# Modulation rows of the first layer norm in three blocks instead of four, with the last key group accumulating in the bank that holds their products

## Chip, cores, metric

One core of one Trainium2 chip runs the whole kernel. The metric is device time in microseconds (us), the median of a kernel's executions. The 27 executions of the kernel before that were run beside the experiments lie within 0.25% (838.13 to 840.25 us). "Span" is the time from the first to the last instruction in the profile of one execution; it is about 2 us shorter than the measured time (on average 1.80 us for the kernel before, 2.01 for the changed one).

## The reference, cut to what matters

```python
# x: 2048 x 1024 bf16; c: 1 x 1024; w_mod: 1024 x 6144; wqkv: 1024 x 3072
mod = (silu(c) @ w_mod).reshape(1, 6, 1, 1024)
sa, ca, ga, sb, cb, gb = (mod[:, i] for i in range(6))
h = layernorm(x) * (1 + ca) + sa          # needs two sixths of w_mod
q, k, v = split(h @ wqkv)                  # 32 heads of 32
x = x + ga * (linear_attention(phi(q), phi(k), v) @ wo)
h = layernorm(x) * (1 + cb) + sb
x = x + gb * ((silu(h @ w_gate) * (h @ w_up)) @ w_down)
```

The change concerns the first 31 us alone: from the first loads to the end of the K products of the first 512 rows of x.

## The kernel before

In this stretch one queue of loads brings, in this order, four tiles of x, the columns of `w_mod` for scale (`ca`) and shift (`sa`), and the K half of `wqkv`: 7 MiB. `w_mod` comes in four blocks ("phases") of 2, 3, 2 and 1 columns of 128. Each phase ends with a "row step", which turns its products into scale and shift, and with a scaling of the transposed x. Only then can the K products of these columns run. There are eight K groups (4 row tiles by 2 halves), each of which adds up 8 columns in a PSUM bank of its own.

```python
    PH = [(0, 2), (2, 5), (5, 7), (7, 8)]
    ...
    load_wme(0, 0, DC); load_wk(0, 2)
    load_wme(1, 0, 4); load_wme(1, 4, 8); load_wk(2, 3); load_wk(3, 5)
    load_wme(2, 0, 4); load_wme(2, 4, 8); load_wk(5, 6); load_wk(6, 7)
    load_wme(3, 0, DC); load_wk(7, 8)
    ...
    # 128x1 products into bank 7, column 2*cc + kind
    nc.tensor.matmul(bank[7][:, o:o + 1], lhsT=wme[:, j, col:col + P], rhs=scT[:, j:j + 1], ...)

    def mod_rows(c0, c1):
        nc.vector.tensor_copy(out=m1[:, 1, c0:c1], in_=bank[7][:, 2 * c0:2 * c1:2])
        nc.vector.tensor_copy(out=saT[:, c0:c1], in_=bank[7][:, 2 * c0 + 1:2 * c1 + 1:2])
        nc.vector.tensor_scalar_add(out=ca1T[:, c0:c1], in0=m1[:, 1, c0:c1], scalar1=1.0)
    ...
    kblk(range(7), 2)                     # groups 0-6, column 2
    kblk(range(7), 3)
    mod_mm(2, 0, 0, 4); mod_mm(2, 1, 0, 4)
    kblk(range(4), 4)
    mod_mm(2, 0, 4, 8); mod_mm(2, 1, 4, 8)
    mod_finish(2); modulate_phase(2)
    kblk(range(4, 7), 4); kblk(range(7), 5); kblk(range(4), 6)
    mod_mm(3, 0, 0, DC); mod_mm(3, 1, 0, DC)
    mod_finish(3); modulate_phase(3)
    spread(nc.vector, scT[:])
    kblk(range(4, 7), 6)
    for cc in range(7):                   # group 7 waits for bank 7 to be free of rows
        kblk((7,), cc)
    for g in range(8):
        kblk((g,), 7)
        k_evac(bank[g], *G[g])
    # then the V groups: banks 0, 1, 2, 3, 4, 0, ...
```

## Time and profile before

| | |
|---|---|
| time, median of 3 | 838.41 us (838.36 to 838.48) |
| span of the profiled execution | 837.0 us |
| first V product | 31.44 us |
| last phase-2 piece of w_mod landed | 22.93 us |
| last wk piece landed | 26.67 us |

Landings are read from the semaphore updates in the trace. First two lines of the page: the span, and the busy time, share and number of instructions of each engine.

```profile
span 837.0 us, 10504 instructions
...
PE 825.1 (99%) x4127; PEld 388.4 (46%) x4207; DVE 351.5 (42%) x660; ACT 150.9 (18%) x288; POOL 80.1 (10%) x147
```

TensorE (PE) is 99% busy, so all there is to win are the few microseconds in which it waits, and the waits that its trace names all come before the first V product's start at 31.44 us. The timeline of TensorE shows them (start, duration, line, shapes, count; in brackets the idle time before and what ended it). L271 is a K product, L367 a modulation product, L286 the first V product.

```profile
17.59 1.69 PE L271 MATMUL bank<-M,M 128*128 128x512 bf16 x7 [0.46 <-DVE M L253]
19.75 1.67 PE L271 MATMUL bank<-M,M 128*128 128x512 bf16 x7 [0.48 <-DMA M<-in_A_wqkv_dram]
...
22.52 0.81 PE L367 MATMUL bank<-scT,M 128*128 128x1 bf16 x16
...
24.24 2.55 PE L271 MATMUL bank<-M,M 128*128 128x512 bf16 x11 [0.24 <-DVE M L253]
26.63 0.54 PE L367 MATMUL bank<-scT,M 128*128 128x1 bf16 x16
27.03 4.04 PE L271 MATMUL bank<-M,M 128*128 128x512 bf16 x18
31.44 2.75 PE L286 MATMUL bank<-M,M 128*128 128x512 bf16 x11 [0.36 <-DVE M L268]
```

One matmul takes 0.38 us in the trace, but the next starts after 0.216 us, so the idle time in brackets is smaller than the time in which nothing was started.

The chain of waits (start, duration, what) is followed back from the end of the kernel:

```profile
14.85 8.09 DMA M<-in_w_mod_dram
...
22.98 0.37 PE bank L367 x8
...
23.37 0.16 DVE m L373
...
23.77 0.42 DVE M L253
...
24.24 2.55 PE bank L271 x11
26.79 0.38 PE bank L367 x16
27.17 2.41 PE bank L271 x11
...
30.69 0.70 DVE M L268
...
31.44 0.59 PE bank L286 x2
```

The chain runs through the landing of the last phase-2 piece of `w_mod` at 22.93 us, the row step (L373 to L375: 0.40 us from its start to the scaling, L253), the rest of the products, and the evacuation of bank 0, for which the first V product waits.

### The profile page before, as it was taken

What the parts mean: (1) busy time and instruction counts of PE and PEld (TensorE: products, weight loads), DVE (VectorE), ACT (ScalarE), POOL (GpSimd) and SP (SyncE); (2) the same over time, 40 slices, a digit from 0 to 9 for tenths busy, and PEclk for the clock granted to TensorE, in tenths of its full rate; (3) what the DMA queues carried; (4) which work ended last, traced back from release to release, by engine and by line L of the source; (5) the groups of instructions that cost most, each with busy time, mean ns of one, the idle gap of its engine ahead of it and who ended that gap; (6) DMA issues with size and microseconds to landing.
All of it is one profiled execution on the core that took longest, in us unless ns stands there. A gap on an engine that the chain in (4) does not pass through costs nothing.

```text
span 837.0 us, 10504 instructions
## 1 busy us (share of the span) xinstructions
PE 825.1 (99%) x4127; PEld 388.4 (46%) x4207; DVE 351.5 (42%) x660; ACT 150.9 (18%) x288; POOL 80.1 (10%) x147
## 2 busy tenths in 40 slices
PE   8999999999999999999999999999999999999998
PEld 4454544544444444444444444444444444444445
DVE  5678889788656655344552012222101111111011
ACT  4335533323211111111110001111000111100000
POOL 2034310032222223100000000000000000000000
PEclk9999999999999999999999999999999999999999
DMA  9987888155588987998884225555313555211220
GB/s 290 314 169 137 137 177 213 41 136 126 145 216 220 214 238 200 244 284 239 251 260 124 76 72 153 156 154 153 102 66 94 152 153 152 73 38 45 76 70 26
DMA packets 232625, 129.41 MB, mean 155 GB/s; under 512 B 89728, under 2 KB 218752, under 8 KB 232576
## 3 DMA queue, kind: packets, MB, share of 16 engines
q1 hardware_dynamic: 182224, 97.01, 42.7%
q10 hardware_dynamic: 48048, 23.34, 12.9%
q0 software_dynamic: 2304, 8.39, 2.6%
q8 instruction: 33, 0.54, 0.3%
q14 instruction: 16, 0.13, 0.1%
HBM read 95.42 MB, written 12.58 MB: 129 GB/s over the span
## 4 chain that ended last, share of the span: by engine, by line
PE 96%; SPq 2%; DMA 1%; issue 1%; DVE 0%; ACT 0%
PE bank L555 23%; PE bank L574 23%; PE bank L549 23%; PE bank L286 7%; PE bank L506 7%; PE bank L294 7%; PE bank L271 6%; DMA M<-in_w_mod_dram 1%; PE bank L479 1%; PE bank L303 1%; SPq L144 1%; SPq L147 1%; SPq L137 0%; PE bank L367 0%; DVE M L268 0%
## 5 line engine op out<-in xcount | busy, mean ns | idle before, releaser
L555 PE MATMUL bank<-M,M 128*128 128x512 bf16 x881 | 210.4, 379 | 0.8
L549 PE MATMUL bank<-M,M 128*128 128x512 bf16 x875 | 209.9, 379 | 1.1
L557 DVE TENSOR_TENSOR M<-bank,e 128x512 bf16<-128x512 f32 x112 | 77.5, 692 | 249.0 <-PE bank L555 237.5
L574 PE MATMUL bank<-M,M 128*128 128x512 bf16 (+2 forms) x715 | 146.9, 362 | 0.6
L552 ACT ACTIVATE e<-bank 128x512 f32<-128x512 f32 x112 | 66.8, 597 | 439.6 <-PE bank L549 404.5
L574 PEld LDWEIGHTS <-M 128*128 128x128 bf16 x952 | 90.9, 98 | 103.0
L555 PEld LDWEIGHTS <-M 128*128 128x128 bf16 x896 | 87.7, 98 | 105.7
L549 PEld LDWEIGHTS <-M 128*128 128x128 bf16 x896 | 87.3, 98 | 103.8
L577 DVE TENSOR_TENSOR M<-bank,M 128x512 bf16<-128x512 f32 (+2 forms) x34 | 22.5, 661 | 169.9 <-PE bank L574 153.8
L271 PE MATMUL bank<-M,M 128*128 128x512 bf16 x248 | 56.8, 379 | 2.6 <-DVE M L253 1.6
L506 PE MATMUL bank<-M,M 128*128 128x512 bf16 x251 | 57.6, 379 | 0.3
L294 PE MATMUL bank<-M,M 128*128 128x512 bf16 x248 | 56.6, 379 | 0.4
L286 PE MATMUL bank<-M,M 128*128 128x512 bf16 x251 | 55.6, 379 | 0.6 <-DVE M L268 0.4
L266 ACT ACTIVATE e<-bank 128x512 f32<-128x512 f32 x64 | 37.3, 596 | 91.7 <-PE bank L294 52.8
L574 PE MATMUL bank<-M 128*128 128x512 bf16 x219 | 50.7, 379 | 0.3
L268 DVE SCALAR_TENSOR_TENSOR M<-bank,e 128x512 bf16<-128x512 f32 x64 | 44.3, 692 | 3.9
L326 DVE CUSTOM_DVE_ANT_0 M<-M,sc_bc 128x1024 f32<-128x1024 bf16 x32 | 40.1, 1252 | 0.4
L286 PEld LDWEIGHTS <-M 128*128 128x128 bf16 x256 | 25.0, 98 | 30.8 <-issue 0.6
L506 PEld LDWEIGHTS <-M 128*128 128x128 bf16 x256 | 25.0, 98 | 29.8
L271 PEld LDWEIGHTS <-M 128*128 128x128 bf16 x256 | 24.1, 98 | 30.8 <-DVE M L253 3.3
L267 DVE TENSOR_SCALAR e<-e 128x512 f32<-128x512 f32 x64 | 29.0, 453 | 21.2 <-ACT e L266 21.2
L294 PEld LDWEIGHTS <-M 128*128 128x128 bf16 x256 | 24.6, 98 | 27.9
(71 smaller groups left out, 339.9 us busy)
## 6 DMA issues: line engine op xcount, KB each, us to landing
M<-in_B_w_gate_dram SPq DMA_DIRECT2D x56, 512.0 KB, 3.9
M<-in_B_w_up_dram SPq DMA_DIRECT2D x56, 512.0 KB, 4.9
x_scratch<-M POOLq DMA_DIRECT2D x16, 512.0 KB, 5.5
M<-x_scratch ACTq DMA_DIRECT2D x16, 512.0 KB, 3.5
M<-in_B_w_down_dram SPq DMA_DIRECT2D x6, 1024.0 KB, 8.3
M<-in_A_x_dram SPq DMA_DIRECT2D x16, 256.0 KB, 4.1
M<-in_A_wqkv_dram SPq DMA_DIRECT2D x4, 1024.0 KB, 11.1
M<-in_A_x_dram ACTq DMA_DIRECT2D x16, 256.0 KB, 4.0
```

Source lines behind the costliest of these rows:

```text
L266: nc.scalar.activation(out=e[:], in_=acc, func=ACT.Exp)
L268: nc.vector.scalar_tensor_tensor(out=dst, in0=acc, scalar=0.0, in1=e[:], op0=ALU.max, op1=ALU.add)
L271: nc.tensor.matmul(acc[:], lhsT=M4[:, sc_, cc, t * P:(t + 1) * P], rhs=wk[:, cc, h * NB:(h + 1) * NB], start=(cc == 0), stop=(cc == DC - 1))
L286: nc.tensor.matmul(acc[:], lhsT=M4[:, sc_, cc, t * P:(t + 1) * P], rhs=wv[:, cc, h * NB:(h + 1) * NB], start=(cc == 0), stop=(cc == DC - 1))
L294: nc.tensor.matmul(acc[:], lhsT=wq[:, cc, qc * P:(qc + 1) * P], rhs=M4[:, sc_, cc, :], start=(cc == 0), stop=(cc == DC - 1))
L326: nc.vector.tensor_tensor_reduce(out=prod.rearrange("p (j k) -> p j k", j=DC), in0=rowT[i][:, :, b, :], in1=sc_bc[:].rearrange("p (j k) -> ...
L506: nc.tensor.matmul(acc[:], lhsT=oTs[st % 3][:, cc, :], rhs=wo[:, cc, hs], start=(cc == 0), stop=(cc == DC - 1))
L549: nc.tensor.matmul(g_ps[:], lhsT=wg_blk[:, cc, fs], rhs=M4[:, sc_, cc, :], start=(cc == 0), stop=(cc == DC - 1))
L552: nc.scalar.activation(out=sg[:], in_=g_ps[:], func=ACT.Silu)
L555: nc.tensor.matmul(u_ps[:], lhsT=wu_blk[:, cc, fs], rhs=M4[:, sc_, cc, :], start=(cc == 0), stop=(cc == DC - 1))
L557: nc.vector.tensor_tensor(out=gus[sc_][:, f, :], in0=u_ps[:], in1=sg[:], op=ALU.mult)
L574: nc.tensor.matmul(y_ps[:, 0:w], lhsT=gus[sc_][:, f, t * P:(t + 1) * P], rhs=wd(f)[:, c0:c1], start=(f == 0), stop=(f == FC - 1))
```

## The change

Its intent: one row step less, no small last block, a shorter row step (one add in float32), K group 7 no longer left to the end but kept in step by sharing bank 7 with the modulation products, the last columns group by group so that evacuation starts early, and some products of zeros ("fill", "warm") in places where TensorE waits. The diff, cut to its core:

```diff
-    PH = [(0, 2), (2, 5), (5, 7), (7, 8)]
+    PH = [(0, 2), (2, 5), (5, 8)]
     ...
-    load_wk(3, 5)
+    load_wk(3, 4)
+    load_wk(4, 5)
     load_wme(2, 0, 4)
     load_wme(2, 4, 8)
     load_wk(5, 6)
-    load_wk(6, 7)
-    load_wme(3, 0, DC)
-    load_wk(7, 8)
+    load_wk(6, 8)
     ...                                   # one_zero: float32, 1 0 1 0 ...
+        nc.vector.tensor_tensor(out=modT[:, o0:o1], in0=bank[7][:, N7 + o0:N7 + o1], in1=one_zero[:, o0:o1], op=ALU.add)
     ...
+    def fill(n):                          # N7 = 384; zeros onto unused columns of bank 7
+        for _ in range(n):
+            nc.tensor.matmul(bank[7][:, N7 + 2 * DC:NB], lhsT=zt[:, 0:P], rhs=zt[:, N7 + 2 * DC:NB], ...)
+    def kmm7(cc, part):                   # group 7: 384 columns at once, the last 128 at the end
+        c0, c1 = (N7, NB) if part else (0, N7)
+        nc.tensor.matmul(bank[7][:, c0:c1], lhsT=M4[:, 0, cc, 3 * P:4 * P], rhs=wk[:, cc, NB + c0:NB + c1], ...)
     ...
+    kblk(range(8), 2)
+    kblk(range(8), 3)
+    kblk(range(3), 4)
     mod_mm(2, 0, 0, 4)
     mod_mm(2, 1, 0, 4)
-    kblk(range(4), 4)
+    kblk(range(3, 6), 4)
     mod_mm(2, 0, 4, 8)
+    fill(6)
     mod_mm(2, 1, 4, 8)
     mod_finish(2)
     modulate_phase(2)
     ...                                   # phase 3 and the late group 7 removed
+    kblk(range(6, 8), 4)
     for g in range(8):
-        kblk((g,), 7)
+        for cc in range(5, 8):
+            kblk((g,), cc)
+        if g == 7:
+            for cc in range(DC):
+                kmm7(cc, 1)
         k_evac(bank[g], *G[g])
```

Left out: the same treatment of phases 0 and 1, five added warm-up products, and the first normalization moved ahead of half of another tile's statistics.

More of the change, by code (lines that the diff above doesn't have):

```diff
@@ L176 @@
     nc.gpsimd.memset(den_eps_t[:], DEN_EPS)
-    saT = const.tile([P, DC], BF16, name="saT")
-    ca1T = const.tile([P, DC], BF16, name="ca1T")
+    modT = const.tile([P, 2 * DC], F32, name="modT")
+    ca1T, saT = modT[:, 0::2], modT[:, 1::2]
+    one_zero = const.tile([P, 2 * DC], F32, name="one_zero")
+    nc.gpsimd.memset(one_zero[:], 0.0)
+    nc.gpsimd.memset(one_zero[:, 0::2], 1.0)
     sbT = const.tile([P, DC], BF16, name="sbT")
@@ L359, in tr0_evac @@
             nc.vector.tensor_copy(out=dst, in_=tp)
+    N7 = 384
     def mod_mm(p, kind, j0, j1):
@@ L364, in mod_mm @@
             for cc in range(c0, c1):
-                o = (2 * cc) + kind
+                o = N7 + 2 * cc + kind
                 col = (0 if kind else D) + cc * P
                 nc.tensor.matmul(bank[7][:, o:o + 1], lhsT=wme[:, j, col:col + P], rhs=scT[:, j:j + 1],
-                                 start=(not kind and j == 0 and cc == c0),
-                                 stop=(kind == 1 and j == DC - 1 and cc == c1 - 1),
-                                 skip_group_check=True)
-    def mod_rows(c0, c1):
-        nc.vector.tensor_copy(out=m1[:, 1, c0:c1], in_=bank[7][:, 2 * c0:2 * c1:2])
-        nc.vector.tensor_copy(out=saT[:, c0:c1], in_=bank[7][:, 2 * c0 + 1:2 * c1 + 1:2])
-        nc.vector.tensor_scalar_add(out=ca1T[:, c0:c1], in0=m1[:, 1, c0:c1], scalar1=1.0)
-    def mod_finish(p):
-        mod_rows(*PH[p])
+                                 start=(p == 0 and kind == 0 and j == 0 and cc == c0),
+                                 stop=(kind == 1 and j == DC - 1 and cc == c1 - 1), skip_group_check=True)
+    def mod_finish(p):
+        o0, o1 = 2 * PH[p][0], 2 * PH[p][1]
+        nc.vector.tensor_tensor(out=modT[:, o0:o1], in0=bank[7][:, N7 + o0:N7 + o1], in1=one_zero[:, o0:o1], op=ALU.add)
+    def fill(n):
+        for _ in range(n):
+            nc.tensor.matmul(bank[7][:, N7 + 2 * DC:NB], lhsT=zt[:, 0:P], rhs=zt[:, N7 + 2 * DC:NB],
+                             start=False, stop=True, skip_group_check=True)
+    def kmm7(cc, part):
+        c0, c1 = (N7, NB) if part else (0, N7)
+        nc.tensor.matmul(bank[7][:, c0:c1], lhsT=M4[:, 0, cc, 3 * P:4 * P], rhs=wk[:, cc, NB + c0:NB + c1],
+                         start=(part == 1 and cc == 0), stop=(cc == DC - 1), skip_group_check=True)
     def modulate_phase(p, c0=0, c1=SCW):
@@ L393 @@
     ln_stats_act(1)
-    ln_stats(2)
-    ln_xn(0, nc.vector)
+    ln_stats(2, lambda: ln_xn(0, nc.vector))
     tr0(0)
     tr0_evac(0)
-    warm(2)
+    warm(4)
     ln_stats(3, lambda: ln_xn(1, nc.vector))
@@ L402 @@
     ln_xn(2, nc.vector)
+    warm(2)
     mod_mm(0, 0, 0, DC)
@@ L407 @@
     tr0_evac(2)
+    warm(1)
     modulate_phase(0, 0, 2 * P)
@@ L419, in kblk @@
         for g in gs:
-            kmm(bank[g], 0, G[g][0], G[g][1], cc)
+            if g < 7:
+                kmm(bank[g], 0, G[g][0], G[g][1], cc)
+            else:
+                kmm7(cc, 0)
     kblk(range(4), 0)
-    kblk(range(1), 1)
     tr0(3)
+    modulate_phase(0, 2 * P, 3 * P)
     tr0_evac(3)
-    kblk(range(1, 4), 1)
-    modulate_phase(0, 2 * P, 4 * P)
+    kblk(range(4), 1)
+    modulate_phase(0, 3 * P, 4 * P)
     kblk(range(4, 6), 0)
@@ L430 @@
     mod_mm(1, 1, 0, 4)
-    kblk(range(6, 7), 0)
-    kblk(range(4, 5), 1)
+    kblk(range(4, 6), 1)
+    fill(6)
     mod_mm(1, 0, 4, 8)
@@ L436 @@
     modulate_phase(1)
-    kblk(range(5, 7), 1)
-    kblk(range(7), 2)
-    kblk(range(7), 3)
+    kblk(range(6, 8), 0)
+    kblk(range(6, 8), 1)
+    kblk(range(8), 2)
+    kblk(range(8), 3)
+    kblk(range(3), 4)
     mod_mm(2, 0, 0, 4)
     mod_mm(2, 1, 0, 4)
-    kblk(range(4), 4)
+    kblk(range(3, 6), 4)
     mod_mm(2, 0, 4, 8)
+    fill(6)
     mod_mm(2, 1, 4, 8)
@@ L446 @@
     modulate_phase(2)
-    kblk(range(4, 7), 4)
-    kblk(range(7), 5)
-    kblk(range(4), 6)
-    mod_mm(3, 0, 0, DC)
-    mod_mm(3, 1, 0, DC)
-    mod_finish(3)
-    modulate_phase(3)
     spread(nc.vector, scT[:])
-    kblk(range(4, 7), 6)
-    for cc in range(7):
-        kblk((7,), cc)
+    kblk(range(6, 8), 4)
     for g in range(8):
-        kblk((g,), 7)
+        for cc in range(5, 8):
[3 more added lines that the diff above has]
+                kmm7(cc, 1)
         k_evac(bank[g], *G[g])
```

## The prediction

> **What bounds the kernel now.** The page gives TensorE 99% busy over 837.0 us. The change touches only the start: by the timeline the first V product (line 286) begins at 31.44 us. The waits of TensorE after that point total 0.4 us (the first V group on VectorE), so the other 805.6 us are one packed, untouched stream: what moves that first V product moves the end by as much. The windows show granted clock 1.00 from 8 us on. [...] the trace agrees (starts 427 ns apart until 3.7 us, then 216); no gap here cools it, so filler products buy no clock.
>
> **Where those 31.4 us go.** From 8.04 (first transpose) to 31.44 there is about 18.8 us of work: 64 K products at 0.216, 32 transposes at 0.056, 128 modulation products at 0.025, two warm-ups. The rest, about 4.6 us, is gaps: 0.5 before the first K product, 0.76 waiting for the second half of phase 0 (transposed tile 3), 0.62 for the phase-1 rows, 0.64 for the load of wk 3–4 (landed 19.71), 0.25 for the last phase-2 w_mod piece (22.93), 0.40 for its rows and scaling, 0.53 for bank 0's evacuation (all eight groups finish together). Underneath, the load queue: 7 MiB by 26.67 us, saturated but for a dip at 22.5–24.5 (170–250 GB/s), when the last phase's 256-byte rows move. [...] the trace agrees, 2135 packets being under 512 bytes there.
>
> **What the change does.**
> 1. Three phases: one row step less, and no 256-byte rows; w_mod 5–7 is needed as one, 1.5 MiB instead of 1.0 before column 5 can start. It should land near 24 us (22.93 before; the fourth phase ended at 26.04), all of wk near 25.7–26.5.
> 2. Rows: three VectorE operations (0.16, 0.15, 0.17; 0.40 from first start to scaling) become one of about 0.16, saving 0.2 per phase. Float32 scalars cost nothing: line 237 already runs with them at 0.54 for 1024 columns.
> 3. Group 7 shares bank 7, so it keeps pace with the others: about 3 to 4 more K products are done early, filling the gaps at 17 and 24 us. Its 8 extra 128-column products cost what the 384-column ones save. Fillers (12 x 0.05) and warm-ups (5 x 0.216) fall mostly in idle time.
> 4. Last columns group by group: evacuations (1.1 per group on VectorE) start early, so the 0.53 wait goes.
> 5. First normalization earlier: first transpose 0.9 earlier, but phase 0 stays bound by tile 1 and w_mod (10.00).
>
> **Sum.** Gaps gained: 0.75 (tile 3) + 0.3 (phase 1) + 0.5 (bank 0) + 0.3 (rows). Lost: 24 K products plus the extra ones (5.6 us) now follow the last w_mod piece. 24.0 + 1.3 + 5.7 gives a first V product near 30.9, 0.5–0.6 earlier.
>
> **Predicted:** 837.8 us, 8 in 10 between 837.0 and 838.7. Faster by over 2%: 0.5%; within: 98.5%; slower: 1%.
>
> **Right or wrong shows in:** the first V product's start (30.3–31.7; the change of time equals its shift); no wait before it; landing of the last w_mod piece (23.5–24.5); busy time after it unchanged; one row operation per phase.
>
> **What would make it wrong:** if that piece lands after 24.4, the gain is gone or negative; if larger rows lift the queue, 1.2 us are gained.

## The result

| | before | changed |
|---|---|---|
| median of 6 executions | 838.41 us (838.22 to 838.58) | 838.39 us (838.16 to 839.9) |
| ratio | | 1.0002, 95% interval 0.9989 to 1.0015 |
| span of the profiled execution | 837.0 us | 837.9 us |

A ratio is the mean time of one kernel's executions over that of the other's of the same rounds, so it is not quite the ratio of the medians.

The profiled execution of the changed kernel is the one of 839.9 us. The page after:

```profile
span 837.9 us, 10546 instructions
...
PE 828.2 (99%) x4153; PEld 390.6 (47%) x4232; DVE 350.5 (42%) x653; ACT 151.6 (18%) x288; POOL 80.2 (10%) x149
```

The same stretch of TensorE's timeline (L273 and L387 are K products, L372 modulation products, L382 fillers, L288 the first V product):

```profile
21.22 0.74 PE L372 MATMUL bank<-scT,M 128*128 128x1 bf16 x24
21.83 0.81 PE L273 MATMUL bank<-M,M 128*128 128x512 bf16 x3
22.71 0.45 PE L372 MATMUL bank<-scT,M 128*128 128x1 bf16 x12
23.02 0.46 PE L382 MATMUL bank<-M 128*128 128x112 bf16 x6
23.88 0.45 PE L372 MATMUL bank<-scT,M 128*128 128x1 bf16 x12 [0.40 <-DMA M<-in_w_mod_dram]
24.59 0.32 PE L387 MATMUL bank<-M,M 128*128 128x384 bf16 x1 [0.26 <-DVE modT L378]
25.04 0.39 PE L273 MATMUL bank<-M,M 128*128 128x512 bf16 x1
25.92 6.08 PE L273 MATMUL bank<-M,M 128*128 128x512 bf16 x20 [0.49 <-DMA M<-in_A_wqkv_dram]
31.84 1.10 PE L387 MATMUL bank<-M,M 128*128 128x384 bf16 x11
32.77 1.46 PE L288 MATMUL bank<-M,M 128*128 128x512 bf16 x6
```

Between 17 and 21 us TensorE now runs without a gap, and the wait in front of the first V product is gone, as intended. But the waits have moved to 22 to 26 us, and the twenty K products from 25.92 us take 6.08 us where they should take about 4.5 (the last in 0.38, the others one per 0.216). The windows view shows why (duration, then busy time and number of instructions of each engine; then PEclk, the granted clock, DMA share, GB/s):

```profile
18.96:22.38 3.42, 3.42 (x39) 1.82 (x37) 0.00 (x0) 0.00 (x0) 0.00 (x0) 1.00 1.09 339
22.38:25.79 3.41, 2.19 (x34) 1.22 (x34) 1.38 (x5) 0.00 (x0) 0.00 (x0) 1.00 1.08 362
25.79:29.20 3.41, 3.28 (x8) 1.13 (x8) 1.88 (x4) 1.20 (x2) 0.00 (x0) 0.50 1.07 372
...
```

From 25.79 to 29.20 us the clock was at half. That stretch is 3.41 us long; the windows above are cut to its length. It follows a window in which TensorE was busy for only 2.19 of 3.41 us. The 2.19 us are somewhat too low: the trace holds 54 of the 56 K products of groups 0 to 6, and one of the two missing records belongs near 24.2 us. Put in where the next run's trace has it, it makes about 2.44 us, an estimate. My prediction had said that "no gap here cools it, so filler products buy no clock". In this execution the clock did fall, to 0.50, after gaps of under 0.9 us. In the other five the mean clock was 1.000 and the span 836.1 to 836.5 us, so this is an event of some executions and does not by itself explain the missing gain.

The chain of waits after:

```profile
19.15 6.73 DMA M<-in_A_wqkv_dram
...
25.92 6.08 PE bank L273 x20
...
```

The chain now starts at the landing of wk columns 6 and 7 (25.88 us), for which group 0 waits with its column 6, with everything else behind it.

The row step, by VectorE's groups of lines between 8 and 32 us (busy, mean ns of one, idle before), before:

```profile
L375 DVE TENSOR_SCALAR ca1T<-m 128x2 bf16<-128x2 bf16 (+2 forms) x4 | 0.7, 168 | 0.0
L373 DVE CAST m<-bank 128x2 bf16<-128x2 f32 (+2 forms) x4 | 0.6, 162 | 10.1 <-PE bank L367 10.0
L374 DVE CAST saT<-bank 128x2 bf16<-128x2 f32 (+2 forms) x4 | 0.6, 151 | 0.0
```

and after, with the scaling that reads its result:

```profile
L255 DVE TENSOR_SCALAR M<-M,modT 128x512 bf16<-128x512 bf16 (+2 forms) x12 | 3.8, 366 | 0.4 <-ACT M L359 0.2
...
L378 DVE TENSOR_TENSOR modT<-bank,one_zero 128x6 f32<-128x6 f32 (+1 forms) x3 | 0.5, 163 | 9.1 <-PE bank L372 9.1
```

Twelve operations became three of 163 ns. The scaling with float32 scalars costs no more than before: its mean is 366 ns, over a mix that has some narrower pieces.

### The profile page after: what moved, and what is told of

It is laid out like the page before. It is cut to its first block, busy times and chain, and to the rows that moved or that the text cites. A ratio compares the mean times of both kernels' runs of the same rounds, so it can differ in the third digit from the quotient of the medians.

```text
span 837.9 us, 10546 instructions
## 1 busy us (share of the span) xinstructions
PE 828.2 (99%) x4153; PEld 390.6 (47%) x4232; DVE 350.5 (42%) x653; ACT 151.6 (18%) x288; POOL 80.2 (10%) x149
## 4 chain that ended last, share of the span: by engine, by line
PE 96%; DMA 2%; SPq 1%; issue 1%; DVE 0%
PE bank L567 23%; PE bank L586 23%; PE bank L561 23%; PE bank L518 7%; PE bank L288 7%; PE bank L296 7%; PE bank L273 6%; PE bank L491 1%; DMA M<-in_w_mod_dram 1%; PE bank L305 1%; DMA M<-in_A_wqkv_dram 1%; SPq L147 1%; SPq L144 0%; SPq L137 0%; PE bank L387 0%
## 5 line engine op out<-in xcount | busy, mean ns | idle before, releaser
L273 PE MATMUL bank<-M,M 128*128 128x512 bf16 x241 | 56.8, 387 | 1.1 <-DMA M<-in_A_wqkv_dram 0.5
L288 PE MATMUL bank<-M,M 128*128 128x512 bf16 x251 | 55.6, 379 | 0.3
L288 PEld LDWEIGHTS <-M 128*128 128x128 bf16 x256 | 25.0, 98 | 29.9
L273 PEld LDWEIGHTS <-M 128*128 128x128 bf16 x248 | 24.2, 99 | 29.9 <-issue 2.7
```

Source lines behind the costliest of these rows:

```text
L273: nc.tensor.matmul(acc[:], lhsT=M4[:, sc_, cc, t * P:(t + 1) * P], rhs=wk[:, cc, h * NB:(h + 1) * NB], start=(cc == 0), stop=(cc == DC - 1))
L288: nc.tensor.matmul(acc[:], lhsT=M4[:, sc_, cc, t * P:(t + 1) * P], rhs=wv[:, cc, h * NB:(h + 1) * NB], start=(cc == 0), stop=(cc == DC - 1))
```

## The experiments

Theory: before and after, the first V product is bound by late loads, not by TensorE's earlier gaps. Larger blocks make the last needed piece of `w_mod` land later; sharing bank 7 and finishing group by group leave less to do after it; the two cancel. On top of this, the waits that now lie together before 26 us let the clock fall in some executions (one of six so far). Rivals: the half clock alone hides a gain; the larger blocks are the gain and something else loses it.

Eleven runs were made, in three sets, each set on one chip; runs 1, 3 and 6 repeat a kernel. The kernel before was run again beside each set, 27 executions in all: median 838.47 us, 838.13 to 840.25, two of them with mean clock under 0.9985 (839.72 and 840.25 us).

### 1. The changed kernel again

No edit. Expected:

> The changed kernel again. Theory (clock): the half-clock stretch of 3.4 us in the one profiled execution (25.8 to 29.2 us) is an occasional event; executions without it show mean clock 1.000, a span of 836.1 to 836.5 us and a first V product near 31.0 us; one with it is about 1.6 us longer and shows 0.998. Rival (fixed): the half-clock stretch belongs to the kernel and comes in every profile; then most executions show 0.998.

Measured: 838.51 us (838.02 to 838.9) beside 838.35 us for the kernel before (runs 1, 2, 4 and 5 share these executions of it), ratio 1.0000 (0.9988 to 1.0013), all five at clock 1.000, spans 836.0 to 836.8 us. Over both sets one of eleven executions had the half-clock stretch, and the ten others have no gain either. In the trace of this run, TensorE at full clock from the same wait on:

```profile
25.53 0.39 PE L273 MATMUL bank<-M,M 128*128 128x512 bf16 x1
26.41 4.48 PE L273 MATMUL bank<-M,M 128*128 128x512 bf16 x20 [0.48 <-DMA M<-in_A_wqkv_dram]
30.72 1.10 PE L387 MATMUL bank<-M,M 128*128 128x384 bf16 x11
31.65 2.54 PE L288 MATMUL bank<-M,M 128*128 128x512 bf16 x11
```

The same twenty products take 4.48 us instead of 6.08, so the stretch costs 1.6 us. But all loads landed about half a microsecond later than in the first profile (wk 6 and 7 at 26.36), and the first V product, at 31.65 us, came later than in the profile of before. The expected position near 31.0 missed for that reason; the spread of the spans also went up to 836.8. The first rival falls: without the half clock there is no gain either.

### 2. Without fillers

```diff
-    fill(6)        # twice
-    warm(4)        # after the first transposed tile
+    warm(2)
-    warm(2)        # before the phase-0 products
-    warm(1)        # before the first K product
```

> The changed kernel without its 12 filler products and its 5 added warm-ups. Theory (the fillers hold the clock): half-clock stretches come in more executions than the one in six seen so far, at least half of them, each costing 1.5 us or more: median 839 us or above. Rival (my prediction's words, fillers buy no clock): the same share of executions as with them, time within 0.3 us of the changed kernel.

Measured: 838.62 us (838.22 to 840.01), ratio 1.0007 (0.9994 to 1.0019). Three of five executions show clock 0.998 (840.01, 839.63, 838.62). The median expected by the theory was not reached, since one of the three cost nothing visible (span 836.6). Where the half clock lay in the executions that were not profiled is not known. The windows of its profile, cut at the bounds of its own half-clock stretch:

```profile
22.92:26.34 3.42, 2.17 (x27) 1.01 (x24) 1.82 (x5) 0.00 (x0) 0.00 (x0) 1.00 1.09 360
26.34:29.75 3.41, 3.41 (x10) 1.22 (x8) 2.47 (x5) 1.79 (x3) 0.00 (x0) 0.50 1.06 376
```

Again the half-clock window follows one with 2.17 of 3.42 us busy.

### 3. The same once more, for the count

> The changed kernel without fillers and added warm-ups once more, for the count of half-clock stretches, which came in 3 of 5 executions without them and 1 of 11 with them. Theory (fillers hold the clock): 2 to 5 of 5 again show 0.998. Rival (chance): none or one.

Measured: 838.17 us (837.88 to 840.97), ratio 1.0002 (0.9988 to 1.0016); two of five at clock 0.998, one of them with 840.97 us, the other with 838.17. Together 5 of 10 without fillers against 1 of 16 with them (the changed kernel and the next run). If the kernels did not differ in this, five or more of the six would fall on the ten by chance once in 54 times. Its profile was undisturbed. One window of that length near its loads:

```profile
23.79:27.21 3.42, 2.56 (x22) 1.17 (x21) 2.11 (x6) 0.86 (x2) 0.00 (x0) 1.00 1.10 356
```

Busy for 2.56 of 3.42 us, the clock held. This window too lacks the record of a product near 24.0 us; with it, it was about 2.81 us (an estimate). The clock fell after 2.17 us in run 2, whose trace is complete, and after about 2.44 in the changed kernel's profile, with its missing record put in.

The busy time of such a stretch does not tell it all: from 22.26 to 25.67 us this run was busy for only 1.93 us, about 2.18 with the missing record, as little as run 2 in the window before its clock fell (2.17), and here the clock held. What made the difference was not shown.

### 4. More fillers

```diff
     kblk(range(3, 6), 4)
+    fill(8)
     mod_mm(2, 0, 4, 8)
-    fill(6)
+    fill(16)
     mod_mm(2, 1, 4, 8)
     ...
     kblk(range(6, 8), 4)
+    busy(4)            # four 128-column products of zeros, added to bank 5
```

> The changed kernel with more filler products in the three waits at 22 to 25 us (8 before and 16 in place of 6 between the parts of the last modulation products, 4 of 128 columns after them). Theory (clock): no execution shows a clock under 1.000; the times of all executions lie together, at the undisturbed executions of the changed kernel plus at most 0.3 us. Rival (the half clock is not tied to activity): about one in six still shows it.

Measured: 838.57 us (838.28 to 838.61), ratio 1.0001 (0.9988 to 1.0015), all five at clock 1.000, within 0.33 us of each other. The window in question:

```profile
22.42:25.83 3.41, 3.18 (x58) 2.42 (x56) 1.32 (x5) 0.00 (x0) 0.00 (x0) 1.00 1.09 368
```

With the counts of run 3 (clock 0.998 in 5 of 10 executions without fillers, in 1 of 16 with them), fillers steady the clock here. They do not make the kernel faster than before. (In this profile the wait for wk 6 and 7 is still there: they landed at 25.70 us, and the twenty products began at 25.75.)

### 5. Column 5 of all groups first

```diff
+    kblk(range(8), 5)
     for g in range(8):
-        for cc in range(5, 8):
+        for cc in range(6, 8):
             kblk((g,), cc)
```

> The changed kernel with column 5 of all eight groups done before columns 6 and 7 group by group. Theory (late load): the gap of 0.67 us in front of group 0's column 6, for the load of wk 6 and 7 that landed at 25.88 us, goes; first V product 0.5 to 0.7 us earlier in executions at full clock; also the half-clock stretch gets rarer. Rival (that load is not what is waited for): the gap stays, no change.

Measured: 837.85 us (837.68 to 837.93), ratio 0.9993 (0.9980 to 1.0005), all five at clock 1.000. The gap went, and the first V product came at 30.59 us.

### 6. The same on another chip

> Column 5 first once more, on another chip if it falls so, for the size of its gain and the count of half-clock stretches: 0.5 us under the kernel before (0.3 to 0.7), 0 of 5 executions under clock 1.000. If the half-clock stretch is as likely as in the changed kernel (1 of 11), one in five may still show it.

Measured: 837.58 us (837.44 to 838.22) beside 838.65 us for before, ratio 0.9990 (0.9977 to 1.0002), all five at 1.000; 1.07 us, more than the 0.3 to 0.7 expected. Its timeline:

```profile
24.72 1.69 PE L273 MATMUL bank<-M,M 128*128 128x512 bf16 x7
...
26.41 3.19 PE L273 MATMUL bank<-M,M 128*128 128x512 bf16 x14
...
30.20 4.05 PE L288 MATMUL bank<-M,M 128*128 128x512 bf16 x18
```

The eight column-5 products, which need only wk 5, now fill the wait for wk 6 and 7. Nine of the ten executions of this version are below every one of the 27 of before (838.13 and up), the tenth at 838.22. Both intervals just include 1; the gain is 0.5 us on one chip and 1.1 on the other.

### 7. One add, alone

The kernel before, with `modT`, `one_zero` and the single `tensor_tensor` in place of the three row operations; nothing else.

> The kernel before with one part of the change: scale and shift kept in float32, one add in place of three row operations. Theory (my prediction's step 2): each row step is 0.2 us shorter from its first start to the scaling; only the one after the last phase-2 piece is on the path, so the first V product comes 0.2 us earlier and the time falls by 0.2 us. Rival: the load of the next pieces decides, no change (under 0.1 us).

Measured: 838.33 us (838.1 to 838.61) beside 838.57, ratio 0.9995 (0.9982 to 1.0009): 0.24 us, the expected size, but inside the scatter. The profile decides it better, in the table below: from the landing to the first V product 8.31 us instead of 8.51. (All loads of that run landed 0.7 us earlier, so its first V product came at 30.52 us, and 0.56 us were given back at 167 us, when one load of x took 1.5 us to issue on the queue of ScalarE, 0.35 to 0.45 in every other profile.)

### 8. Three blocks, alone

The kernel before with the new `PH` and the new order of loads, phase 3 removed; rows and groups as before.

> The kernel before with another part alone: three blocks of w_mod, groups and rows as before. Theory (late load): the last w_mod piece lands near 23.9 us and 29 K products plus the 0.5 us wait for bank 0 follow it: first V product near 31.7 us, time 0.2 to 0.5 us longer than the kernel before. Rival (larger rows and one step less are the gain): first V product earlier than 31.2 us, time shorter.

Measured: 839.62 us (838.59 to 839.94) beside 838.57, ratio 1.0008 (0.9996 to 1.0021), all at clock 1.000. Its chain of waits:

```profile
15.31 8.09 DMA M<-in_w_mod_dram
...
31.61 2.53 PE bank L285 x11
```

The last piece landed at 23.40 us and the first V product came at 31.61, near the expected 31.7: the second rival falls. The loss in the median, 1.05 us, is larger than I expected. The profiled execution is the fastest of the five (span 836.8, the others to 838.1); what the slower ones waited for was not profiled and stays open.

### 9. Four blocks with the rest of the change

```diff
-    PH = [(0, 2), (2, 5), (5, 8)]
+    PH = [(0, 2), (2, 5), (5, 7), (7, 8)]
     ...                                # loads of wk 6, phase 3 and wk 7 as before
     kblk(range(6, 8), 4)
+    kblk(range(8), 5)
+    mod_mm(3, 0, 0, DC); mod_mm(3, 1, 0, DC); mod_finish(3); modulate_phase(3)
+    kblk(range(8), 6)
     for g in range(8):
-        for cc in range(5, 8):
-            kblk((g,), cc)
+        kblk((g,), 7)
```

> The changed kernel with the four blocks of before (2, 3, 2, 1 columns) and, as group 7 now keeps pace, column 7 alone done group by group. Theory (what follows the last w_mod piece counts, the block change is not the gain): first V product at 30.2 to 30.6 us, as early as with column 5 first, 0.4 to 0.8 us ahead of the changed kernel, mean clock 1.000. Rival (256-byte rows and the fourth row step cost more): first V product at 31 us or later.

Measured: 838.11 us (837.93 to 838.25) beside 838.57, ratio 0.9993 (0.9980 to 1.0005), all at 1.000; first V product at 30.61 us, 0.01 above what was expected. The three-block layout is not needed for the gain.

### 10. The same without the fillers of phase 2

```diff
     mod_mm(2, 0, 4, 8)
-    fill(6)
     mod_mm(2, 1, 4, 8)
```

> The four-block version with group 7 sharing its bank, without the 6 filler products of phase 2, which there fall into work and not into a wait. Theory (TensorE has no load to wait for at 22 to 24 us in this version): first V product 0.3 us earlier than in the four-block version for the same landing times, near 30.3 us; time 0.2 to 0.4 us under it; mean clock stays 1.000[...]. Rival (loads decide there too): no change under 0.1 us.

Measured: 837.95 us (837.24 to 839.64) beside 838.65, ratio 0.9995 (0.9982 to 1.0007), all at 1.000. First V product at 30.41 us with the loads 0.2 us later than in run 9: 0.44 us less after the landing. The fillers did lie on the path there; the medians, of different chips, differ by 0.16 us only, less than I expected. The chain of this run shows a next limit: the first V product now waits for its own weights, which landed at 30.36 us, with TensorE idle for 0.19 us before it. The execution of 839.64 us (span 837.9, clock 1.000) was not profiled and is unexplained.

### 11. Column 5 first, with more fillers

`fill(8)` and `fill(16)` as in run 4, on top of run 5.

> Column 5 first, and more fillers in the two load waits of phase 2 (8 before, 16 in place of 6 between). Theory: fillers fit into the waits (0.3 and 0.6 us) and cost nothing, time within 0.1 us of column 5 first, all executions at clock 1.000. Rival (fillers delay the modulation products): 0.2 us or more longer.

Measured: 838.47 us (837.56 to 838.83) beside 838.65, ratio 1.0000 (0.9986 to 1.0013), all five at 1.000, and 0.9 us above run 6 of the same set. The rival holds:

```profile
22.89 0.44 PE L372 MATMUL bank<-scT,M 128*128 128x1 bf16 x12
23.20 0.95 PE L382 MATMUL bank<-M 128*128 128x112 bf16 x16
23.98 0.44 PE L372 MATMUL bank<-scT,M 128*128 128x1 bf16 x12
```

The piece had landed at 23.09 us, 0.4 us earlier than in run 6, but the products that need it stood behind sixteen fillers until 23.98.

### The runs side by side

"Landed": the last piece of `w_mod` that column 5 needs. "After it": first V product minus landing.

| kernel | landed | first V | after it |
|---|---|---|---|
| before | 22.93 | 31.44 | 8.51 |
| one add alone (7) | 22.21 | 30.52 | 8.31 |
| three blocks alone (8) | 23.40 | 31.61 | 8.21 |
| changed again (1) | 24.33 | 31.65 | 7.32 |
| without fillers, again (3) | 23.60 | 30.92 | 7.32 |
| more fillers (4) | 23.67 | 31.00 | 7.33 |
| changed, half clock | 23.83 | 32.77 | 8.94 |
| without fillers, half clock (2) | 23.69 | 32.72 | 9.03 |
| column 5 first (5) | 23.91 | 30.59 | 6.68 |
| column 5 first, again (6) | 23.52 | 30.20 | 6.68 |
| column 5 first, more fillers (11) | 23.09 | 30.61 | 7.52 |
| four blocks, shared bank (9) | 22.66 | 30.61 | 7.95 |
| four blocks, fewer fillers (10) | 22.90 | 30.41 | 7.51 |

The third column repeats to 0.01 us where it could be compared at full clock: runs 5 and 6 of one program (6.68), and runs 1, 3 and 4, which differ in fillers alone (7.32 to 7.33). Landings move by up to 1.2 us among the nine profiles with the same loads (23.09 to 24.33). That is why single times say so little here, and this column so much. The two half-clock rows stand 1.6 to 1.7 us above 7.32.

## Why the prediction was right or wrong

- **Total.** 837.8 us predicted, range 837.0 to 838.7; measured 838.39. The range held, but it also holds the time of the kernel before (838.41), so that it held says nothing for the mechanism. The forecast gain of 0.6 us did not come.
- **"What moves that first V product moves the end by as much": right up to the last matmul, wrong for the end.** From the first V product to the end of the last matmul, 802.4 us passed in every profile but one (run 7, with the give-back told there). From there to the end of the span it took 3.14 us in the kernel before and in run 7, 3.06 to 3.07 in runs 9 and 10, and 2.75 to 2.77 in all nine profiles with three blocks. At the end SyncE waits for the semaphores of its transfers one after the other, 0.06 us each. The last store lands 1.80 or 1.81 us after the last matmul in all of them, but seven more waits follow its own in the first group, six in the second and one in the third. These issue 231, 232 and 229 transfers on SyncE's queue, so the place of the last store seems to follow their number; no run tests that. The change thus has about 0.4 us that the prediction did not look for.
- **The landing, "should land near 24 us": right** (23.83; 23.1 to 24.3 in all three-block runs). The mean of the four runs with a small phase 2 is 22.68 us, that of the nine with three blocks 23.67: the larger block costs 1.0 us at this point, in these single executions.
- **"24.0 + 1.3 + 5.7": the term after the landing was mis-sized.** I put 7.0 us there; at full clock it is 7.32. The piece left out is the wait of group 0 for wk 6 and 7, 0.67 us without a start before 25.92 us. I had predicted their landing (25.7 to 26.5; it was 25.88) but not held it against the moment when group 0 would ask for them. Doing column 5 first takes 0.64 us off that term (6.68), which shows it; the rest of the term was put 0.3 us too large.
- **"0.5–0.6 earlier": counted from one late execution.** The 31.44 us are those of a profile with a span of 837.0 us; the median of the 27 executions is 836.7. An estimate of the usual first V product is the median span less 802.4 us and less the piece after the last matmul: 31.16 us before. So about 0.3 us of the forecast gain was not there to win, and the mis-sized term is the other 0.3.
- **What the change was worth.** By the profiles, landing 1.0 us later, 1.2 us less after it (8.51 to 7.32): 0.2 us gained. By the estimate from the spans, the changed kernel's first V product came at 31.30 us (836.45, the ten executions at full clock), so 0.1 us later than before. The piece after the last matmul gives 0.4 us, and 0.2 are lost outside the span (below): together nothing, as measured. The change as a whole trades one for the other. Run 8 has the first half alone and is slower in the median; runs 9 and 10 have the second without the first and are faster in the median.
- **"Gaps gained: 0.75 + 0.3 + 0.5 + 0.3": wrong as a sum.** The gaps at 13 to 20 us did close in the changed kernel's profile (run 1 still waits 0.64 us at 18.2 us for a load), but they were not on the chain of waits. Work done earlier only meant that TensorE stood waiting at 22 to 26 us for the same loads. Of the four, the row step after the last piece counted (run 7), and by the chain of waits the one for bank 0, which no run tests by itself.
- **"Saving 0.2 per phase": right,** and only once on the path (8.51 to 8.31 in run 7). Float32 scalars cost nothing, as said: the six 128x512 scalings take 409 ns each before and after.
- **"First transpose 0.9 earlier": not seen.** It began at 7.30 to 8.61 us in the ten profiles with the moved normalization, at 7.59 to 8.04 in the three without. The prediction had it off the path; why it did not move was not looked into.
- **"Filler products buy no clock": wrong.** A mean clock of 0.998 came in 5 of 10 executions without fillers, in 1 of 16 with them; the half-clock stretch cost 1.6 us where TensorE had twenty products to do (6.08 us instead of 4.48). I had looked for a long gap. The windows of 3.41 us before the two falls had 2.19 us (about 2.44 with the missing record) and 2.17 us of busy time in them and no gap over 0.9 us.
- **What lies outside the span.** Measured time less span averages 1.80 us for the 27 executions of before and 2.01 us for the eleven of the changed kernel; all versions with the shared bank show 1.99 to 2.08, three blocks alone 1.82, one add alone 1.95. So about 0.2 us, as much as the gain within the span, is lost where the profile does not look. Its cause stays open.
- **"If larger rows lift the queue, 1.2 us are gained": half right.** The last wk piece lands at 25.7 us on average in the nine three-block runs, at 26.7 in the four four-block ones, so the queue was lifted by 1.0 us; whether by the 256-byte rows that went or by the fewer issues, no run separates. The trace of before shows two stretches: at 22.2 to 24.3 us, with 1779 of 1815 packets under 512 bytes, the DMA engines were busy throughout (share 1.02) and moved 242 GB/s (371 in the changed kernel); at 24.3 to 25.5 us they were busy for 0.59 of the time and moved 114 (350). For the last piece of `w_mod` it did not help, since that comes before these in the queue.

The best version found is the changed kernel with column 5 first.

## What to carry to other kernels

A gap of the busiest engine is worth something only if the chain of waits passes through it; otherwise filling it moves the wait to the next load, here from 17 to 21 us to 22 to 26 us. When transfers are the bound, compare versions by the time from the landing of the last needed piece to the first dependent step, which repeated far better here than the total (6.68 us twice, where the medians of runs 5 and 6 were 837.85 and 837.58 us), and order the remaining work by when its inputs land. Waits of less than a microsecond that lie close together came before a fall of the clock in two profiles here (about 2.44 and 2.17 us of busy time in the 3.41 us before it), and in the changed kernel the fall cost 1.6 us: keep the array fed there, but with fillers sized to the wait (in run 11 sixteen of them held up the next products until 23.98 us, though their piece had landed at 23.09), or better with real products moved into it (0.64 us less after the landing in runs 5 and 6).

## What the traces show besides

- Both half-clock stretches that were profiled lasted 3.41 us: 25.79 to 29.20 us in the changed kernel, 26.34 to 29.75 us in run 2. One of 11 executions of the changed kernel and 5 of 10 without fillers had a mean clock of 0.998. Why some executions of one program are hit and others not was not shown.
- Sharing bank 7 costs a wait: in the complete trace of run 1, group 7's product starts 0.39 us after the one before it, not 0.216, in each of the two places where it follows a row step on bank 7. (The wait of 0.26 us shown for it in the changed kernel's profile is too long, since the record of the product before is missing there.)
